# Linear attention beside a top-8 MLP on one core: q computed token-major and transposed by DMA, M built mostly in one pass, first outputs copied out by ScalarE

## The chip, the cores and the metric

The kernel runs on one core of one Trainium2 chip. The metric is the device time of one execution, in microseconds (us); lower is better. Inside the core, TensorE (PE in the profile, its weight loads PEld) multiplies, VectorE (DVE), ScalarE (ACT) and GpSimd (POOL) do elementwise work, and SyncE (SP) issues most of the DMAs. Matmul results land in PSUM, in eight banks of 128 x 512 float32.

## The reference, cut to what matters

The input x has 2048 tokens of 640 columns. The output is `x + A(layernorm(x)) + B(layernorm(x))`.

```
# A: linear attention, 32 heads of 20 columns
q, k, v = split(xn @ wqkv)                 # [32 heads, 2048, 20] each
phi(t) = where(t > 0, t + 1, exp(t)) + 1e-6
kv  = sum_s phi(k)[s]^T v[s]               # one 20 x 20 block per head
z   = sum_s phi(k)[s]
num = phi(q) @ kv ;  den = phi(q) . z + 1e-6
A   = concat_heads(num / den) @ wo
# B: eight tokens, chosen by r, go through an MLP
r = xn @ w_r ;  idx = the 8 largest of r
y = (silu(xn[idx] @ w_gate) * (xn[idx] @ w_up)) @ w_down * sigmoid(r[idx])
B = xn, with y added to the rows idx
```

## The kernel before, in words

Tokens are worked in 16 tiles of 128 (`T = 16`); the 640 columns are five groups of 128 (`KC = 5`). There is no scheduler: the order on each engine is the order in which the code is written, and each engine works through its own list in order. SP's list is the DMA queue of nearly all transfers. Buffers are tiles of pools; an instruction that writes a PSUM tile waits for the instructions that read that tile before, and the waits are made per tile, not per column.

**Start.** Ten wide matmuls on zeros (`warm_mm`, L271) run while the first tokens arrive. Tiles 0 to 2 of the normalised input are transposed by PE, tiles 3 to 15 by DMA (`ln_norm`, L196: `xnT<-xn`).

**Loop over tiles.** For tile t PE does `k_mm` (token-major, matmuls of 512 and 129 columns, L236), `ga_mm(t - 1)` (three matmuls into the running sum G = xn^T phi(k), L259) and `q_mm` (L248: 25 matmuls of 128 columns, weights as the stationary operand with a column step of 5, so that q comes out already transposed, [column, token]). ScalarE takes exp and relu of k and q from PSUM, VectorE joins them to phi: `pk` for k (token-major) and `pqT` for q (transposed, written straight by VectorE, L225). `late_loads(t)` puts one weight load per tile on SP; `keep` writes finished rows of `x + xn` to a DRAM buffer `xcp` (L363).

**After the loop.** PE transposes r for the top-8 search (`pr`, L428), sums phi(k) over the tokens (`z_mm`, L460), continues G in `gb1` (L489), merges the top-8 candidates (`pc`, L499), and when `gb1` is through it forms the denominators (`pden`, L571) from `pqT` and `zm`. `zm` holds z spread over heads; z gets from rows to partitions by four small DMAs (`zrel`, L477). ScalarE turns den into 1/den (`rden`, L580, L581); it goes to DRAM in four copies and back as `rb`, and VectorE multiplies `pqT` by it in four blocks of 512 tokens (`norm(j)`, L632). Between these stand the MLP's first half (`gu`, L606), the last part of G (`gb2`, L590), the head blocks of kv (`pkv`, L659, evicted under a mask by VectorE, L670) and the MLP's second half (`py`, L688). `py` is scattered into `xcp` by an indirect DMA (L697), and `x_sb` is read back from there in six pieces (L702).

**M.** M = kv @ wo is built in five row groups m (L728). Each needs two passes over wo, of even and odd blocks of 80 rows, in four 32-column strips of PE; each M group is copied to SBUF by ScalarE or VectorE (L737).

**Outputs.** For each tile, ten matmuls (five groups m, columns 0 to 511 and 512 to 639, L743), an add of `x_sb` by VectorE straight from PSUM (L751), and a DMA to the output. Four PSUM accumulators take turns: three pairs of banks and the two single banks D0 and D1.

Of the kernel before, what the change touches and what calls it, by code (L numbers as in the profile page):

```python
# [25 lines left out]
PAD = 16  # L26
# [3 lines left out]
WARM = 10  # L30
LAST = (0, 320, 512, 640)
# [13 lines left out]
def kernel(  # L45
# [47 lines left out]
    kvT = sb([EB, PAD + NEB * KC * 2 * PAD], BF16, "kvT")  # L93
# [4 lines left out]
    rscr = dram.tile([NTB * P, TBLK], BF16, name="rscr")  # L98
# [32 lines left out]
    headg = sb([P, NTB, H], BF16, "headg")  # L131
    nc.vector.memset(headg[:], 1.0)
    mask80 = sb([EB, KC, 4, 4], BF16, "mask80")
# [20 lines left out]

    head_select(headg[:], [(0, NTB), (-4, H)], 1, 4)
# [87 lines left out]

    def q_mm(t, tag="B"):
        ps = pair(tag, f"q{t}")
        for m in range(KC):
            for kc in range(KC):
                nc.tensor.matmul(  # L248
                    ps[:, m * P : (m + 1) * P],
                    lhsT=wq[:, kc, m::KC],  # L250
                    rhs=xnT[:, kc, t * P : (t + 1) * P],
                    start=(kc == 0 and m in (0, 4)), stop=(kc == KC - 1),
                    skip_group_check=True,
                )
        return ps
# [47 lines left out]
    def small_consts(t):  # L303
        if t == 3:
            for j in range(4):
                nc.gpsimd.affine_select(
                    out=cmask[:], in_=cmask[:], compare_op=ALU.not_equal, fill=1.0,
                    base=-32 * j, pattern=[[-1, C]], channel_multiplier=1,
                )
        elif t == 4:  # L310
            nc.gpsimd.affine_select(
                out=selm[:], in_=selm[:], compare_op=ALU.not_equal, fill=1.0,
                base=0, pattern=[[-1, NTB]], channel_multiplier=1,
            )
            nc.gpsimd.iota(iota_i[:], pattern=[[1, 32]], base=0, channel_multiplier=0)
            nc.gpsimd.tensor_copy(iof[:], iota_i[:])
        elif t == 5:
            nc.gpsimd.iota(prt_i[:, 0:1], pattern=[[0, 1]], base=4 * S, channel_multiplier=1)
            nc.gpsimd.iota(prt_i[:, 1:2], pattern=[[0, 1]], base=0, channel_multiplier=TBLK)
            nc.gpsimd.tensor_copy(prt[:], prt_i[:])  # L320
            nc.gpsimd.tensor_copy(boff[:], prt[0:NTB, 1:2])
        elif t == 6:
            head_select(mask80[:], [(0, KC), (-DH, 4), (0, 4)], 1, DH)
# [17 lines left out]
    def late_loads(t):  # L341
        def part(dst, src, a, b):
            nc.sync.dma_start(dst[:, a:b, :], src[:, a:b, :])

        wv_v = wqkv_v[:, :, 2 * D : 3 * D]
        plan = {
            2: (x_sb, x_v, 8, 12), 5: (x_sb, x_v, 12, 16),
            6: (wg, kcF, 0, 2), 7: (wg, kcF, 2, 4), 8: (wg, kcF, 4, 5),
            9: (wu, kcU, 0, 2), 10: (wu, kcU, 2, 4), 11: (wu, kcU, 4, 5),
            12: (wv, wv_v, 0, 2), 13: (wv, wv_v, 2, KC), 14: (wo, wo_v, 0, 4), 15: (wo, wo_v, 4, 8),  # L350
            16: (wd, kcD, 0, 6), 17: (wd, kcD, 6, 12),
        }
        if t in plan:
            part(*plan[t])

# [12 lines left out]
    def q_phi(t, er):  # L368
        phi_vec(pqT[:, :, t * P : (t + 1) * P], er, True)
# [72 lines left out]
    nc.vector.max(cand[:, 0, :], rT[:])  # L442
    nc.vector.max_index(idxu[:], cand[:, 0, :], rT[:])
# [13 lines left out]
    def z_mm(t):  # L457
        i = t % 4
        for a, b in ((0, TBLK), (TBLK, D)):
            nc.tensor.matmul(  # L460
                zp[32 * i : 32 * i + 32, a:b],
                lhsT=ones_bf[:],
                rhs=pk[:, t, a:b],
                start=(t < 4), stop=(t >= T - 4),
                tile_position=(0, 32 * i),
            )
# [5 lines left out]
    zpart = sb([P, D], F32, "zpart", tag="rb")  # L472
    nc.scalar.copy(zpart[:], zp[:, 0:D])
# [6 lines left out]
    late_loads(T)  # L480
    late_loads(T + 1)
# [25 lines left out]
    for t in range(4, T):  # L507
        gb1(t)
# [22 lines left out]
    q_phi(T - 1, qer)  # L531
# [4 lines left out]
    for c in range(C):  # L536
# [7 lines left out]
        out=zm[:], in0=headg[:, 0, :].unsqueeze(1).to_broadcast([P, KC, H]),  # L544
# [19 lines left out]
    keep(T - 4, T)  # L564
    nc.scalar.copy(GT[:, 3:5, 0:TBLK], two(gbA[:]))
# [15 lines left out]
    nc.scalar.activation(rden[:], lden[:], AF.Exp, scale=-1.0)  # L581

# [14 lines left out]

    for t in range(2):
        gb2(t)
# [3 lines left out]
    for a, w in enumerate((wg, wu)):  # L603
# [15 lines left out]
    rb = sb([P, S], BF16, "rb")  # L619

    nc.sync.dma_start(
        rscr[:].rearrange("(p r) n -> p r n", r=4), rden[:].unsqueeze(1).to_broadcast([P, 4, TBLK])
    )
    for j in (0, 2):
        nc.sync.dma_start(
            rb[:, j * TBLK : (j + 2) * TBLK].rearrange("p (j n) -> p j n", j=2),
            rscr[j * P : (j + 2) * P, :].rearrange("(j p) n -> p j n", j=2),
        )

    def norm(j):  # L630
        sl = pqT[:, :, j * TBLK : (j + 1) * TBLK]
        nc.vector.tensor_tensor(  # L632
            out=sl, in0=sl,
            in1=rb[:, j * TBLK : (j + 1) * TBLK].unsqueeze(1).to_broadcast([P, KC, TBLK]),
            op=ALU.mult,
        )

    for t in range(2, 12):
# [9 lines left out]
    for t in range(12, T):  # L648
        gb2(t)
    nc.scalar.copy(GT[:, :, TBLK:D], gbC[:, 0:D].rearrange("p (c f) -> p c f", c=KC))  # L650


    pkv = (bank("D0", "pkv0"), bank("D1", "pkv1"), pair("B", "pkv2"))
    groups = ((0, 2, 4), (1, 3, 5), (6, 7))

    def kv_mm(i):
        for n, b in enumerate(groups[i]):
# [9 lines left out]
    def kv_evict(i):  # L667
        n, w = len(groups[i]), KC * 2 * PAD
        lo, step = groups[i][0], groups[i][1] - groups[i][0]
        nc.vector.tensor_tensor(  # L670
            out=kvT[:, PAD : PAD + NEB * w].rearrange("e (b m c) -> e b m c", b=NEB, m=KC)[
                :, lo : groups[i][-1] + 1 : step, :, 0:PAD
            ],
            in0=pkv[i][0:EB, 0 : n * EB].rearrange("e (b c m) -> e b m c", b=n, m=KC),
            in1=mask80[:].rearrange("e m h j -> e m (h j)").unsqueeze(1).to_broadcast([EB, n, KC, PAD]),
            op=ALU.mult,
        )

    for i in range(3):
        kv_mm(i)  # L680
        kv_evict(i)
# [21 lines left out]

    M = sb([P, KC, D], BF16, "M", tag="wq")
    halves = ((0, TBLK), (TBLK, D))

    class Acc:
        def __init__(self, tag, name):
            if tag == "D":
                self.banks = bank("D0", name + "a"), bank("D1", name + "b")  # L710
                self.spans = halves
            else:
                self.banks = (pair(tag, name),)
                self.spans = ((0, D),)
# [7 lines left out]
    for m in range(KC):  # L722
        pm = Acc("CBADC"[m], f"M{m}")
        for a, b in halves:
            for i in range(2):
                for g in range(4):
                    o = PAD + ((2 * g + i) * KC + m) * 2 * PAD - i * PAD
                    nc.tensor.matmul(  # L728
                        pm.at(a, b)[32 * g : 32 * g + 32, :],
                        lhsT=kvT[:, o : o + 2 * PAD],  # L730
                        rhs=wo[:, 2 * g + i, a:b],
                        start=(i == 0), stop=(i == 1),
                        tile_position=(0, 32 * g),
                    )
        copy = nc.vector.tensor_copy if m in (2, 4) else nc.scalar.copy
        for a, b in pm.spans:
            copy(M[:, m, a:b], pm.at(a, b))  # L737
    norm(1)
    norm(2)


    def out_mm(t, ps, m, a, b):
# [4 lines left out]
            start=(m == 0), stop=(m == KC - 1),  # L747
# [5 lines left out]
    for t in range(T):  # L753
        o_t = work.tile([P, D], BF16, tag=("ek", "rk", "eq", "rq")[t % 4], name=f"o_t{t}")
        if t < T - 1:
            po = Acc("BADC"[t % 4], f"o{t}")
            for m in range(KC):
# [5 lines left out]
            if t == 4:  # L763
                norm(3)
        else:
            for i in range(3):
                a, b = LAST[i : i + 2]
                ps = pair("CBA"[i], f"o_last{i}")[:, 0 : b - a]
                for m in range(KC):
# [37 lines left out]
```

## Time and profile before

| | |
|---|---|
| median of 3 runs | 111.77 us (111.38 to 111.93) |
| the profiled execution: time | 111.62 us |
| its span, first to last instruction | 109.9 us |
| PE busy share of the span | 96% |
| DVE, ACT, POOL busy share | 78%, 50%, 34% |
| DMA: bytes moved, mean rate | 23.09 MB, 210 GB/s |
| granted PE clock | 1.00 |

The profile comes from one execution; the 1.7 us between its span and its time are start and end of the program. Times in the views are counted from the span's first instruction. Matmuls overlap in their pipeline, so the mean duration of one (381 ns for 512 columns) is longer than the distance between two; that distance is read from the chain of waits.

### The profile page before, as it was taken

The numbers are of one execution on the slowest core, as the hardware profiler recorded it, in microseconds if no ns is written. First come the engines' busy times: TensorE is split into PE (matmuls) and PEld (weight loads), VectorE is DVE, ScalarE is ACT, GpSimd is POOL, SyncE is SP. The second block draws the span as 40 slices with busy tenths as digits, with TensorE's granted clock in tenths as the row PEclk, the third lists the DMA queues.
The fourth block names the chain that finished last, engine by engine and source line by source line (L and its number), as shares of the span: only waits on it lengthen the run. The fifth ranks groups of instructions, "written<-read, shape, count | busy, mean of one in ns | idle before, by whom it ended". The sixth has DMA issues, their size and how long they took to land.

```text
span 109.9 us, 2999 instructions
## 1 busy us (share of the span) xinstructions
PE 105.5 (96%) x1183; PEld 69.3 (63%) x1183; DVE 86.1 (78%) x205; ACT 55.1 (50%) x102; POOL 37.9 (34%) x83
## 2 busy tenths in 40 slices
PE   6998999999999999999999999999999999999990
PEld 2456866777577766777667744447995555555560
DVE  6889999887999889875999896951348967698680
ACT  4037987778867797777977745068028000000000
POOL 5414195989889955770000000240008100000000
DMA  2998164930569999998859970899541289997333
GB/s 72 335 375 292 33 36 75 283 66 3 118 177 321 220 267 280 316 305 224 290 187 285 292 257 5 232 378 372 175 145 51 15 228 323 340 387 277 128 119 119
DMA packets 25358, 23.09 MB, mean 210 GB/s; under 512 B 10624, under 2 KB 24064, under 8 KB 25344
## 3 DMA queue, kind: packets, MB, share of 16 engines
q1 hardware_dynamic: 22784, 20.43, 66.5%
q10 hardware_dynamic: 2384, 2.43, 6.4%
q8 instruction: 9, 0.15, 0.6%
q0 software_dynamic: 176, 0.04, 0.6%
q14 instruction: 5, 0.04, 0.1%
HBM read 14.94 MB, written 5.81 MB: 189 GB/s over the span
## 4 chain that ended last, share of the span: by engine, by line
PE 76%; DVE 10%; POOL 8%; issue 3%; DVEq 0%; POOLq 0%
PE o L743 14%; PE k L236 13%; PE q L248 13%; PE gbA L489 6%; PE gaC L259 5%; PE warm L271 4%; PE gbC L590 4%; POOL sq L176 3%; DVE st L163 2%; PE gaD L259 2%; DVE pk L225 2%; PE M L728 2%; POOL sc L178 2%; DVE xn L191 2%; PE gu L606 2%
## 5 line engine op out<-in xcount | busy, mean ns | idle before, releaser
L248 PEld LDWEIGHTS <-wq 128*128 128x128 bf16 x400 | 24.2, 117 | 3.4
L236 PE MATMUL k<-wk,xnT 128*128 128x512 bf16 (+1 forms) x160 | 24.8, 301 | 0.3 <-ACT xnT L206 0.3
L248 PE MATMUL q<-xnT,wq 128*128 128x128 bf16 x400 | 24.9, 220 | 0.0
L743 PEld LDWEIGHTS <-pqT 128*128 128x128 bf16 x165 | 12.8, 98 | 9.3
L236 PEld LDWEIGHTS <-xnT 128*128 128x128 bf16 x160 | 12.3, 98 | 8.5 <-ACT xnT L206 0.9
L213 ACT ACTIVATE eq<-q 128x640 bf16<-128x640 f32 x16 | 11.2, 703 | 10.5 <-PE q L248 10.5
L225 DVE SCALAR_TENSOR_TENSOR pk<-ek,rk 128x640 bf16<-128x640 bf16 x16 | 13.2, 824 | 3.6 <-ACT rk L216 3.4
L743 PE MATMUL o<-M,pqT 128*128 128x512 bf16 x110 | 15.8, 300 | 0.0
L176 POOL TENSOR_TENSOR sq<-sq,half 128x1 bf16<-128x1 bf16 x16 | 12.5, 778 | 6.2 <-DVE sc L175 4.0
L163 DVE BATCH_NORM_STATS2 st<-x_sb 128x6 f32<-128x320 bf16 x32 | 14.1, 480 | 0.4 <-DMA x_sb<-in_A_x_dram 0.4
L225 DVE SCALAR_TENSOR_TENSOR pqT<-eq,rq 128x640 bf16<-128x640 bf16 x16 | 13.2, 823 | 0.7 <-ACT rq L216 0.7
L213 ACT ACTIVATE ek<-k 128x640 bf16<-128x640 f32 x16 | 11.3, 705 | 1.6 <-PE k L236 0.4
L751 DVE TENSOR_TENSOR o_t<-o,x_sb 128x640 bf16<-128x640 f32 x11 | 8.8, 820 | 3.3 <-DMA x_sb<-xcp 1.7
L216 ACT ACTIVATE rq<-q 128x640 bf16<-128x640 f32 x16 | 11.2, 700 | 0.0
L216 ACT ACTIVATE rk<-k 128x640 bf16<-128x640 f32 x16 | 11.2, 699 | 0.0
L259 PE MATMUL gaC<-pk,xn 128*128 128x512 bf16 x32 | 9.5, 378 | 0.2 <-DVE pk L225 0.2
L537 POOL COPY xsT<-xnT 128x5 bf16 x8 | 1.9, 312 | 21.7 <-DVE icol L551 21.7
L178 POOL TENSOR_TENSOR sc<-sq,neg 128x1 f32<-128x1 bf16 x12 | 8.6, 716 | 0.9
L191 DVE TENSOR_SCALAR xn<-x_sb,sc 128x640 bf16<-128x640 bf16 (+2 forms) x17 | 6.9, 412 | 1.2 <-POOL sc L179 1.0
L489 PE MATMUL gbA<-pk,xn 128*128 128x512 bf16 x32 | 7.3, 380 | 0.0
L360 DVE TENSOR_TENSOR x_sb<-x_sb,xn 128x640 bf16<-128x640 bf16 x16 | 7.0, 482 | 0.0
L259 PEld LDWEIGHTS <-xn 128*128 128x128 bf16 x48 | 4.0, 97 | 4.1 <-issue 0.4
(152 smaller groups left out, 120.4 us busy)
## 6 DMA issues: line engine op xcount, KB each, us to landing
xcp<-x_sb SPq DMA_DIRECT2D x4, 640.0 KB, 5.2
x_sb<-in_A_x_dram SPq DMA_DIRECT2D x3, 640.0 KB, 4.7
wd<-in_B_w_down_dram SPq DMA_DIRECT2D x2, 960.0 KB, 6.6
x_sb<-xcp SPq DMA_DIRECT2D x3, 640.0 KB, 6.8
wg<-in_B_w_gate_dram SPq DMA_DIRECT2D x2, 768.0 KB, 6.6
wu<-in_B_w_up_dram SPq DMA_DIRECT2D x2, 768.0 KB, 5.3
out_dram<-o_t ACTq DMA_DIRECT2D x8, 160.0 KB, 2.7
out_dram<-o_t SPq DMA_DIRECT2D x7, 160.0 KB, 3.4
```

Source lines behind the costliest of these rows:

```text
L163: nc.vector.bn_stats(out=stat[t][:, h, :], in_=x_sb[:, t, h * HW : (h + 1) * HW])
L176: nc.gpsimd.tensor_tensor(out=sq[:, 1:2], in0=sq[:, 0:1], in1=half[:], op=ALU.pow)
L178: nc.gpsimd.tensor_tensor(out=sc[:, 1:2], in0=sq[:, 1:2], in1=neg1[:], op=ALU.pow)
L191: nc.vector.tensor_scalar(out=xn[:, t, a:b], in0=x_sb[:, t, a:b], scalar1=sc[:, 0:1], scalar2=sc[:, 1:2], op0=ALU.subtract, op1=ALU.mult,)
L213: nc.scalar.activation(e[:], ps[:, 0:D], AF.Exp)
L216: nc.scalar.activation(r[:], ps[:, 0:D], AF.Relu)
L225: nc.vector.scalar_tensor_tensor(out=dst, in0=ea, scalar=1.0, in1=ra, op0=ALU.min, op1=ALU.add)
L236: nc.tensor.matmul(ps[:, a:b], lhsT=xnT[:, kc, t * P : (t + 1) * P], rhs=wk[:, kc, a:b], start=(kc == 0), stop=(kc == KC - 1),)
L248: nc.tensor.matmul(ps[:, m * P : (m + 1) * P], lhsT=wq[:, kc, m::KC], rhs=xnT[:, kc, t * P : (t + 1) * P], start=(kc == 0 and m in (0, 4)) ...
L259: nc.tensor.matmul(gaC[:, c * TBLK : (c + 1) * TBLK] if c < 2 else gaD[:], lhsT=xn[:, t, c * P : (c + 1) * P], rhs=pk[:, t, 0:TBLK], start ...
L489: nc.tensor.matmul(gbA[:, (c - 3) * TBLK : (c - 2) * TBLK], lhsT=xn[:, t, c * P : (c + 1) * P], rhs=pk[:, t, 0:TBLK], start=(t == 0), stop ...
L743: nc.tensor.matmul(ps, lhsT=pqT[:, m, t * P : (t + 1) * P], rhs=M[:, m, a:b], start=(m == 0), stop=(m == KC - 1),)
```

## The change

- **q.** `q_mm` makes q token-major, like k: for each of the five groups the normalised tile is the stationary operand, and `wq` is streamed in 512 and 128 columns. `regroup` orders the columns: of each head of 20 the first 8, the next 8 and the last 4, so that column groups 0 to 3 hold eights of 16 heads each and group 4 the fours of all heads. The streamed operand is therefore read in runs of 8 (or 4) elements at a step of 20. phi(q) goes to a buffer `pq` (three of them), and SP transposes it by DMA into `pqT`: 16 more DMA transposes. `z_mm` streams `pk` in the same order.
- **Order.** phi of q's last tile moves ahead in VectorE's list, into the search for candidates. `pden` stands after `gb1` of tile 12 (`DEN_AT = 13`), and `gb1` of tiles 13 to 15 follows it. The loads of `wv` move to tiles 8 and 11, those of `wd` from behind the loop to tiles 12 and 13. Two of the four `zrel` DMAs stay on SP, two go on ScalarE's queue.
- **Reciprocals.** `rden` goes to DRAM once, and `rb` is read back in three partition orders, 12 DMAs of 128 x 512; `rb` shares the buffer of `xnT`. `norm(j)` takes two multiplications.
- **kv and M.** kv comes in two groups of four blocks, each evicted in three VectorE instructions. M's groups 0 to 3 take one pass, group 4 two, in the order 0, 2, 1, 3, 4. Groups 0 and 2 share the pair of banks C; the last 128 columns of groups 0 to 3 lie in the second bank of pair A beside group 1's 512 columns; group 4 has pair B.
- **Outputs.** The accumulator of tiles t with t mod 4 = 0 is bank D1 and columns 640 to 767 of pair B; with t mod 4 = 3 it is bank D0 and columns 0 to 127 of the same pair B; the others are the pairs C and A. The first five tiles (`NPRE = 5`) are copied out by ScalarE, and VectorE adds `x_sb` in SBUF.

```diff
     def q_mm(t, tag="B"):
         ps = pair(tag, f"q{t}")
-        for m in range(KC):
-            for kc in range(KC):
+        for kc in range(KC):
+            for rhs, a, b in regroup(wq[:, kc, :]):
                 nc.tensor.matmul(
-                    ps[:, m * P : (m + 1) * P],
-                    lhsT=wq[:, kc, m::KC],
-                    rhs=xnT[:, kc, t * P : (t + 1) * P],
+                    ps[:, a:b],
+                    lhsT=xnT[:, kc, t * P : (t + 1) * P],
+                    rhs=rhs,
...
+    def regroup(ap):
+        v = ap.rearrange("p (h e) -> p h e", e=DH)
+        main = v[:, :, 0 : 2 * E8].rearrange("p h (c d) -> p c h d", c=2)
+        return (main, 0, TBLK), (v[:, :, 2 * E8 : DH], TBLK, D)
...
     def q_phi(t, er):
-        phi_vec(pqT[:, :, t * P : (t + 1) * P], er, True)
+        pq = work.tile([P, D], BF16, tag="pq", name=f"pq{t}", bufs=3)
+        phi_vec(pq[:], er, False)
+        nc.sync.dma_start_transpose(pqT[:, :, t * P : (t + 1) * P], pq[:])
...
-            12: (wv, wv_v, 0, 2), 13: (wv, wv_v, 2, KC), 14: (wo, wo_v, 0, 4), 15: (wo, wo_v, 4, 8),
-            16: (wd, kcD, 0, 6), 17: (wd, kcD, 6, 12),
+            12: (wd, kcD, 0, 6), 13: (wd, kcD, 6, 12), 14: (wo, wo_v, 0, 4), 15: (wo, wo_v, 4, 8),
...
+        if t == 8:
+            part(wv, wv_v, 0, 2)
+        elif t == 11:
+            part(wv, wv_v, 2, KC)
...
     nc.vector.max(cand[:, 0, :], rT[:])
+    q_phi(T - 1, qer)
     nc.vector.max_index(idxu[:], cand[:, 0, :], rT[:])
...
-            (nc.sync if i < 3 else nc.scalar).dma_start(
+            (nc.sync if i < 2 else nc.scalar).dma_start(
...
-    for t in range(4, T):
+    for t in range(4, DEN_AT):
         gb1(t)
...
+    for t in range(DEN_AT, T):
+        gb1(t)
+    nc.scalar.copy(GT[:, 3:5, 0:TBLK], two(gbA[:]))
...
+    mC, mA, mB = pair("C", "M02"), pair("A", "M1r"), pair("B", "M4")
+    mD, mE = bank("D0", "M3"), bank("D1", "oX")
+    m_at = (mC, 0), (mA, 0), (mC, TBLK), (mD, 0), (mB, 0)
+    m_rest = tuple((mA, TBLK + m * P) for m in range(4)) + ((mB, TBLK),)
...
+    m_pass(0)
+    m_copy(nc.scalar.copy, 0)
+    m_pass(2)
+    m_copy(nc.scalar.copy, 2)
+    m_pass(1)
+    m_copy(nc.vector.tensor_copy, 1)
+    m_pass(3)
+    m_copy(nc.scalar.copy, 3)
+    m_pass(4, 0)
+    m_pass(4, 1)
...
     class Acc:
-        def __init__(self, tag, name):
-            if tag == "D":
-                self.banks = bank("D0", name + "a"), bank("D1", name + "b")
+        def __init__(self, t):
+            k = t % 4
+            if k in (1, 2):
+                self.banks = (pair("?CA"[k], f"o{t}"),)
+                self.spans = ((0, D),)
+            else:
+                lo = TBLK + P if k == 0 else 0
+                self.banks = (mE if k == 0 else mD)[:], mB[:, lo : lo + P]
                 self.spans = halves
...
+    for t in range(NPRE):
...
+        o_pre[t] = o_tile(t)
+        for a, b in acc[t].spans:
+            nc.scalar.copy(o_pre[t][:, a:b], acc[t].at(a, b))
+    for t in range(NPRE):
+        nc.vector.tensor_tensor(out=o_pre[t][:], in0=o_pre[t][:], in1=x_sb[:, t, :], op=ALU.add)
+        (nc.scalar, nc.sync)[t % 2].dma_start(out_v[:, t, :], o_pre[t][:])
+    norm(3)
```

More of the change, by code (lines that the diff above doesn't have):

```diff
@@ L130 @@
     nc.vector.memset(kvT[:], 0.0)
[L131 to L133 removed]
+    headm = sb([P, KC, NV, HV], BF16, "headm")
+    nc.vector.memset(headm[:], 0.0)
+    for m in range(4):
+        nc.vector.memset(headm[:, m, m % 2, :], 1.0)
+    nc.vector.memset(headm[:, 4], 1.0)
+    mask80 = sb([EB, 4, E8], BF16, "mask80")
     nc.vector.memset(mask80[:], 1.0)
@@ L617, with rb_load, norm @@
     nc.vector.tensor_tensor(out=hm[:], in0=gu[:, TBLK : TBLK + FJ], in1=hm[:], op=ALU.mult)
[L619 to L627, printed above, removed]
-        )
[L630 to L638, printed above, removed]
+    rb = sb([P, NV + 1, S], BF16, "rb", tag="xnT")
+    def rb_load(j):
+        lo = j * TBLK
+        for v in range(NV + 1):
+            h0, n, r = (v * HV, HV, E8) if v < NV else (0, H, E4)
+            nc.sync.dma_start(
+                rb[:, v, lo : lo + TBLK],
+                rscr[32 * j + h0 : 32 * j + h0 + n, :].unsqueeze(1).to_broadcast([n, r, TBLK]),
+            )
+    nc.sync.dma_start(rscr[:], rden[:])
+    keep(T - 4, T)
+    for j in range(NTB):
+        rb_load(j)
+    def norm(j):
+        js = slice(j * TBLK, (j + 1) * TBLK)
+        sl = pqT[:, 0:4, js].rearrange("p (c v) n -> p c v n", v=NV)
+        nc.vector.tensor_tensor(
+            out=sl, in0=sl, in1=rb[:, 0:NV, js].unsqueeze(1).to_broadcast([P, 2, NV, TBLK]), op=ALU.mult
+        )
+        nc.vector.tensor_tensor(out=pqT[:, 4, js], in0=pqT[:, 4, js], in1=rb[:, NV, js], op=ALU.mult)
+    for t in range(12):
         gb2(t)
@@ L647 @@
     )
[L648 to L654, printed above, removed]
+    pkv = bank("D0", "pkv0"), bank("D1", "pkv1")
     def kv_mm(i):
-        for n, b in enumerate(groups[i]):
+        for n in range(4):
+            b = 4 * i + n
             for kc in range(KC):
@@ L667, in kv_evict @@
     def kv_evict(i):
[L668 to L681, printed above, removed]
+        src = pkv[i][0:EB, 0 : 4 * EB].rearrange("e (b h c) -> e b h c", b=4, h=4)
+        main = kvT[:, 256 * i : 256 * (i + 1)].rearrange("e (b c h d) -> e c b h d", b=4, c=2, h=4)
+        rest = kvT[:, 512 + 128 * i : 512 + 128 * (i + 1)].rearrange("e (b x) -> e b x", b=4)
+        for c in range(3):
+            w = E8 if c < 2 else E4
+            dst = main[:, c] if c < 2 else rest[:, :, 0:16].rearrange("e b (h d) -> e b h d", h=4)
+            nc.vector.tensor_tensor(
+                out=dst, in0=src[:, :, :, c * E8 : c * E8 + w],
+                in1=mask80[:, :, 0:w].unsqueeze(1).to_broadcast([EB, 4, 4, w]), op=ALU.mult,
+            )
+    for t in range(12, 14):
+        gb2(t)
+    kv_mm(0)
+    kv_evict(0)
+    for t in range(14, T):
+        gb2(t)
+    nc.scalar.copy(GT[:, :, TBLK:D], gbC[:, 0:D].rearrange("p (c f) -> p c f", c=KC))
     norm(0)
@@ L767 @@
                 a, b = LAST[i : i + 2]
-                ps = pair("CBA"[i], f"o_last{i}")[:, 0 : b - a]
-                for m in range(KC):
+                ps = (mD, mB, mE)[i][:, 0 : b - a]
+                for m in M_ORDER:
                     out_mm(t, ps, m, a, b)
```

129 lines of the change are left out of this document (79 added, 50 removed).

## The prediction

> **What bounds the kernel now.** I read the page's first and fourth parts, then the chain in order of time, then a table by stretches of time and the groups by shape. First the page: busy shares by engine, and the shares of the chain that ended last.
>
> ```profile
> PE 105.5 (96%) x1183; PEld 69.3 (63%) x1183; DVE 86.1 (78%) x205; ACT 55.1 (50%) x102; POOL 37.9 (34%) x83
> ...
> PE 76%; DVE 10%; POOL 8%; issue 3%; DVEq 0%; POOLq 0%
> ```
>
> PE is busy nearly throughout. The chain (start, duration, what) shows the distance between matmuls, which their own durations hide:
>
> ```profile
> 1.05 4.77 PE warm L271 x13
> ...
> 57.66 1.40 PE q L248 x25
> 59.05 1.38 PE k L236 x10
> ...
> 61.09 1.40 PE q L248 x25
> ...
> 66.60 0.13 PE pc L499
> 66.73 0.02 PE pc L503
> 66.74 5.29 PE gbA L489 x24
> 72.03 1.19 PE pden L571 x20
> ...
> 79.81 1.53 PE pkv L659 x40
> 81.34 0.94 PE py L688 x48
> 82.28 1.63 PE M L728 x48
> ...
> 85.00 2.82 PE o L743 x20
> ```
>
> From tile 6 to the end PE follows PE. So the time falls only where PE gets less work, and rises by every new wait of PE in its own order. PE is not the only full resource. Columns here: stretch, busy time by engine, clock, DMA share, GB/s.
>
> ```profile
> 28.00:30.00 2.00, 1.77 (x13) 0.91 (x11) 2.00 (x4) 1.91 (x4) 1.79 (x7) 1.00 0.71 142
> 31.00:55.20 24.20, 24.20 (x274) 17.63 (x272) 20.70 (x44) 18.57 (x35) 14.28 (x25) 1.00 1.08 272
> 55.20:56.20 1.00, 1.00 (x13) 0.68 (x11) 1.00 (x3) 0.54 (x1) 0.00 (x0) 1.00 0.03 12
> 56.20:65.20 9.00, 9.00 (x114) 5.91 (x113) 8.44 (x17) 6.44 (x13) 0.00 (x0) 1.00 1.02 306
> 69.00:75.50 6.50, 6.50 (x85) 3.16 (x82) 3.76 (x14) 3.19 (x4) 1.94 (x8) 1.00 1.00 332
> 36.30:38.00 1.70, 1.70 (x25) 1.36 (x24) 1.36 (x3) 1.46 (x4) 1.54 (x5) 1.00 1.39 152
> 43.00:46.00 3.00, 3.00 (x37) 2.22 (x35) 2.51 (x6) 2.23 (x6) 2.61 (x4) 1.00 1.11 359
> ```
>
> From 31 to 65 us the DMA engines are full but for one microsecond. Nobody on PE waits for them today, because what they carry is needed late. The change puts 16 transposes and two weight loads into this stretch, and makes PE need the last of them.
>
> **The change part by part.** The sum is made against the profiled execution's 111.62 us, 0.15 below the median of the runs.
>
> *q, gain 0.34.* 25 matmuls at 1.40 become ten like k's, which take 1.38 with one column more; 0.021 by 16 tiles. The streamed operand is now strided. The only strided read in the trace is q's old weight load:
>
> ```profile
> L248 PEld LDWEIGHTS <-wq 128*128 128x128 bf16 x400 | 24.2, 117 | 3.4
> L743 PEld LDWEIGHTS <-pqT 128*128 128x128 bf16 x165 | 12.8, 98 | 9.3
> ```
>
> A step of five elements made it 117 against 98 ns. Were the stream slowed by the same 19%, q would cost 16 x 0.26 = 4.2 us more; below zero it can't cost. Runs of eight are nearer to the contiguous row, so I take nothing. [...]
>
> *M, gain 1.09, then loss of 1.45.* The old M takes 85.00 - 82.28 = 2.72, ten passes of 0.272. The new one has six: 1.63. But the accumulators are shared, and waits are per tile. Pass 2 writes the pair that ScalarE is copying group 0 from; the last 128 columns of pass 3 go to the pair that VectorE copies group 1 from.
>
> ```profile
> L737 ACT CAST M<-M3a 128x512 bf16<-128x512 f32 x1 | 0.6, 585 | 0.2 <-PE M3a L728 0.2
> L737 ACT CAST M<-M3b 128x128 bf16<-128x128 f32 x1 | 0.3, 272 | 0.0
> L751 DVE TENSOR_TENSOR o_t<-o10a,x_sb 128x512 bf16<-128x512 f32 x1 | 0.7, 692 | 0.0
> L751 DVE TENSOR_TENSOR o_t<-o10b,x_sb 128x128 bf16<-128x128 f32 x1 | 0.3, 280 | 0.0
> ```
>
> A copy begins 0.2 after PE's last matmul. First wait: 0.2 + 0.585 + 0.05 for the signal, less 0.06 for the 128 columns that PE still has: 0.78. Second: 0.2 + 0.692 + 0.05 less 0.27: 0.67. M becomes 3.08, a net loss of 0.36.
>
> *Outputs, loss 2.4.* Tiles with t mod 4 of 3 and 0 follow each other and now share pair B. So the second matmul of tiles 4, 8 and 12 waits until the tile before is read out, with ten matmuls queued behind it. At tile 4 ScalarE reads: 0.14 + 0.585 + 0.272 - 0.1 (they overlap) + 0.05, less the 0.22 of the one matmul ahead: 0.73. At 8 and 12 VectorE reads: 0.14 + 0.692 + 0.28 - 0.08 + 0.05 - 0.22, about 0.85 each. Sum 2.43. The old rotation had D0 and D1 as a tile's own banks, and the chain has no such wait. ScalarE's five copies cost nothing: it is idle after M. VectorE must be level again by tile 7 for the 0.85 to hold, and x_sb comes late:
>
> ```profile
> 94.34 0.82 DVE L751 TENSOR_TENSOR o_t<-o,x_sb 128x640 bf16<-128x640 f32 x1 [0.86 <-DMA x_sb<-xcp]
> 95.08 1.48 DVE L632 TENSOR_TENSOR pqT<-pqT,rb 128x2560 bf16<-128x2560 bf16 x1
> ```
>
> Tile 4's rows came 9.3 after the outputs' start at 85.00. Half of kv (0.77) and the longer M (0.36) now stand between py and the outputs, so 8.2. One add (under 0.82), norm(3) at 1.48 and two adds of 0.82 end at about 12.1 or sooner; PE ends tile 7 at 8 x 1.36 + 0.73 = 11.6 and its readout starts 0.2 later. So it holds, barely: each microsecond that x comes later is one more at tile 8.
>
> *The candidates, loss 0.3.* phi of the last q goes before the search ends:
>
> ```profile
> L225 DVE SCALAR_TENSOR_TENSOR pqT<-eq,rq 128x640 bf16<-128x640 bf16 x16 | 13.2, 823 | 0.7 <-ACT rq L216 0.7
> 65.75 0.21 DVE L437 TENSOR_TENSOR candm<-split,selm 4x64 bf16<-4x64 bf16 x1
> 70.18 0.33 DVE L543 TENSOR_TENSOR zm<-headg,zc 128x160 bf16<-128x160 bf16 x1
> 67.69 1.18 SPq L343 DMA_DIRECT2D wd<-in_B_w_down_dram  x2
> 49.51 1.21 SPq L196 DMA_TRANSPOSE xnT<-xn  x1
> ```
>
> The candidates were ready at 65.96, PE took them at 66.60 (pc): 0.64 of cover for 0.82 of new work, and 0.1 for the signal. Queued behind pc stand gb1 and all that follows.
>
> *The denominators, loss 4.0.* They are moved ahead by three tiles of gb1 (5.29/12 = 0.44 each): PE would be there at 72.03 - 1.32 - 0.34 + 0.3 = 70.7. They need the last transposed q and zm, hence zrel, two of whose DMAs stand on SP behind that transpose. Ahead of these in SP's queue: transposes of tiles 4 to 14 and the last one, and both wd. The wd pair is 1.97 MB, at 375 GB/s (between 359 and a full queue) 5.2 us. A transpose moves 0.164 MB. At 359 GB/s that is 0.46; in 28:30 two of them held the engines for 0.71 x 2.0 = 1.42, 0.71 each; in 36.3:38.0 one took the whole 1.7 at 152 GB/s. I take 0.6, between the first two, since most should be queued with others: 12 x 0.6 = 7.2. Against it stand the idle microsecond at 55 and three stretches like 36.3:38.0, which a deeper queue can fill, about 1.1 each: 4.3 in all. The queue then runs dry at 65.2 - 0.3 + 12.4 - 4.3 = 73.0 instead of 65.2; landing and sum over rows 1.1, zm 0.6: 74.7. PE waits 4.0, with gb1, the MLP and all the rest queued behind. Ends: with 0.46 a transpose 2.3; with 1.1 a transpose 10.
>
> [...]
>
> *Answered with one line each.* On SP a transpose takes 1.21 to issue and a load 0.59 (half of the wd row), so a tile's issues are 3.0 us within its 3.43 (61.09 - 57.66); xnT is still made three tiles ahead. GpSimd's extra masks fit, it is idle two thirds of the time. The reciprocals come back in 12 DMAs; norm(0) needs the first three, some 2 us of issues at a load's 0.59, and PE has 9 us of other work between pden's end and M to cover that; without the cover norm(0) would hold the outputs. kv's six evictions instead of three lie under py and the second half of kv.
>
> Sum: 111.62 - 0.34 + 0.36 + 2.43 + 0.3 + 4.0 = 118.4.
>
> **The rivals.**
> - *The queue keeps up*: the transposes slip between the weight loads, as the xnT ones do in 43:46 at 359 GB/s, and nothing is late for the denominators. Then only the PSUM waits are left: 114.4. Against it: share 1.08 over 24 us.
> - *The queue starves the loop*: every pair of transposes behaves like 36.3:38.0. Then even xnT comes late, k waits, and the end slips by 6 more: 124. For it: three such stretches among seven transposes; against it: what is queued behind them could fill the gaps.
> - *The clock falls*: the warm-up's ten matmuls of 512 and three of 128 columns take 4.77 in the chain's first row, 0.44 for 512 columns, where k's ten later take 1.38, 0.22 for 512; so PE runs at half pace when it comes from idling. [...]
> - *Faster*: the waits for shared PSUM are not taken, because the readers are done before PE comes back. It decides at a lag of readout below 0.2 us behind PE; then M and q give 1.43 and the queue keeps up: 110.2. Against it: the copies' own durations above.
> - A change without effect would need losses of 1.4 exactly; I see no mechanism.
>
> **How the numbers follow.** Forecast (denominators late by 2 to 6) 0.50, queue keeps up 0.18, clock falls 0.14, loop starves 0.11, faster 0.04, near no change 0.03. About 0.5%, 0.56 us, is what a measurement can tell from no change. So faster 0.04, same 0.03, slower 0.93. The time is the forecast's, 118.4 on the profiled execution, 118.5 on the median's footing. The range runs from the queue keeping up, 114.4, to just short of the starved loop, 123.
>
> **What would show it.** Right: a wait on PE before pden with a DMA of zrel or pqT as its end; waits of 0.7 to 0.9 at the second matmul of tiles 4, 8, 12; two in M; q at 1.38 a tile. Wrong: pden starting right behind gb1 of tile 12, or q's matmuls further apart than k's, or no gap at tile 8.

## The result, and the profile after

The changed kernel takes 127.65 us (median of 4 runs, 127.47 to 129.24) against 111.69 for the kernel before (111.38 to 111.93): a ratio of 1.146, 95% interval 1.137 to 1.156. The prediction was 118.5, with a range from 114.4 to 123. The profiled execution took 127.47 us with a span of 125.7; that of before, 111.62 with 109.9. The 15.8 us between the spans are what has to be found.

First the page of the changed kernel: busy shares, then the granted clock in 40 slices, then the shares of the chain that ended last, by engine and by line.

```profile
PE 107.4 (85%) x899; PEld 58.9 (47%) x911; DVE 84.7 (67%) x217; ACT 59.9 (48%) x111; POOL 36.8 (29%) x91
...
PEclk9999999999999999999999999559999999999999
...
PE 65%; DMA 13%; DVE 10%; issue 4%; ACT 3%; SPq 2%; ACTq 0%; DVEq 0%
PE k L242 15%; PE q L259 12%; DMA xnT<-xn 9%; PE o L800 7%; PE warm L281 4%; PE gbC L611 4%; DMA zrel<-zpart 3%; PE gaC L269 3%; PE M L800 3%; PE gbA L510 3%; PE oX L800 3%; DVE o_t L809 3%; PE gaD L269 2%; PE pden L589 2%; SPq L389 2%
```

PE was busy for 96% of the span and is now busy for 85%: it waits. DMAs, which had no share of the chain, hold 13% of it, and two slices in the middle show a clock of half speed. Next the chain in order of time (start, duration, what), to be laid beside the rows of before in the prediction.

```profile
55.55 7.10 DMA xnT<-xn
62.66 0.05 issue
62.70 1.56 PE k L242 x10
...
64.91 1.41 PE q L259 x10
66.33 0.32 PE pr L448 x4
...
70.50 0.17 PE pc L520
...
75.42 0.60 SPq L500
76.02 0.05 issue
76.08 4.31 DMA zrel<-zpart
...
81.14 2.52 PE pden L589 x15
83.66 1.37 PE gbA L510 x3
...
94.75 0.36 PE M L747 x4
...
98.07 0.32 PE oX L800
```

And what PE waited for (who waited for whom: us in total, times, longest):

```profile
PE pden L589 <- DVE zm L563: 6.5, 1, 6.5
PE k L242 <- DMA xnT<-xn: 3.3, 4, 1.5
PE M L800 <- DVE o_t L809: 1.5, 2, 0.8
...
PE M L747 <- ACT M L758: 0.6, 1, 0.6
PE M1r L747 <- DVE M L758: 0.6, 1, 0.6
PE M L800 <- ACT o_t L834: 0.6, 1, 0.6
```

One row of before was not shown yet, the start of the transposes of r, which ends the loop:

```profile
62.48 0.32 PE pr L428 x4
```

From these starts the whole difference can be set out by stretches. Three tiles of `gb1` moved from ahead of `pden` to behind it; 1.32 us are moved back for them.

| stretch | before | after | difference | predicted |
|---|---|---|---|---|
| start to `pr` (the loop) | 62.48 | 66.33 | +3.85 | -0.34 |
| `pr` to `pc` | 4.12 | 4.17 | +0.05 | +0.3 |
| `pc` to `pden`, without the three tiles | 4.11 | 10.64 | +6.53 | +4.0 |
| `pden` to M, with the three tiles | 11.57 | 13.61 | +2.04 | 0 |
| M | 2.72 | 3.32 | +0.60 | +0.36 |
| outputs to the end of the span | 24.9 | 27.63 | +2.73 | +2.43 |

The rows add up to 15.80. M and the outputs came nearly as forecast. The loop, the wait for `pden` and the stretch behind it came 8.8 us worse (4.19 + 2.53 + 2.04), and the experiments ask for the cause of these first.

### The profile page after: what moved, and what is told of

Read it like the earlier page. It is cut to its first block, busy times and chain, and to the rows that moved or that the text cites. A ratio compares the mean times of both kernels' runs of the same rounds, so it can differ in the third digit from the quotient of the medians.

```text
span 125.7 us, 2535 instructions
## 1 busy us (share of the span) xinstructions
PE 107.4 (85%) x899; PEld 58.9 (47%) x911; DVE 84.7 (67%) x217; ACT 59.9 (48%) x111; POOL 36.8 (29%) x91
## 3 DMA queue, kind: packets, MB, share of 16 engines
q10 hardware_dynamic: 2528, 2.43, 5.8%
## 4 chain that ended last, share of the span: by engine, by line
PE 65%; DMA 13%; DVE 10%; issue 4%; ACT 3%; SPq 2%; ACTq 0%; DVEq 0%
PE k L242 15%; PE q L259 12%; DMA xnT<-xn 9%; PE o L800 7%; PE warm L281 4%; PE gbC L611 4%; DMA zrel<-zpart 3%; PE gaC L269 3%; PE M L800 3%; PE gbA L510 3%; PE oX L800 3%; DVE o_t L809 3%; PE gaD L269 2%; PE pden L589 2%; SPq L389 2%
## 5 line engine op out<-in xcount | busy, mean ns | idle before, releaser
L259 PE MATMUL q<-wq,xnT 128*128 128x512 bf16 (+1 forms) x160 | 25.2, 303 | 0.0
L242 PEld LDWEIGHTS <-xnT 128*128 128x128 bf16 x160 | 12.2, 98 | 14.5 <-DMA xnT<-xn 4.8
L259 PEld LDWEIGHTS <-xnT 128*128 128x128 bf16 x160 | 12.9, 96 | 11.9
L231 DVE SCALAR_TENSOR_TENSOR pq<-eq,rq 128x640 bf16<-128x640 bf16 x16 | 13.1, 818 | 2.2 <-DMA pqT<-pq 1.5
L800 PE MATMUL o<-M,pqT 128*128 128x512 bf16 (+1 forms) x78 | 12.2, 297 | 0.2
L800 PE MATMUL M<-M,pqT 128*128 128x128 bf16 (+3 forms) x60 | 9.5, 268 | 2.0 <-DVE o_t L809 1.5
L269 PE MATMUL gaC<-pk,xn 128*128 128x512 bf16 x29 | 8.8, 378 | 0.0
L557 POOL COPY xsT<-xnT 128x5 bf16 x8 | 1.1, 210 | 24.6 <-DMA wo<-in_A_wo_dram 24.6
L589 PE MATMUL pden<-pqT,zm 128*32 128x512 bf16 x20 | 2.5, 626 | 6.5 <-DVE zm L563 6.5
L510 PE MATMUL gbA<-pk,xn 128*128 128x512 bf16 x30 | 7.9, 403 | 0.1
L721 POOL DMA_INDIRECT xcp<-y_sb,rowu x1 | 1.8, 1752 | 18.9 <-DVE pqT L659 18.9
```

What stands on the lines that cost most here:

```text
L231: nc.vector.scalar_tensor_tensor(out=dst, in0=ea, scalar=1.0, in1=ra, op0=ALU.min, op1=ALU.add)
L242: nc.tensor.matmul(ps[:, a:b], lhsT=xnT[:, kc, t * P : (t + 1) * P], rhs=wk[:, kc, a:b], start=(kc == 0), stop=(kc == KC - 1),)
L259: nc.tensor.matmul(ps[:, a:b], lhsT=xnT[:, kc, t * P : (t + 1) * P], rhs=rhs, start=(kc == 0), stop=(kc == KC - 1),)
L269: nc.tensor.matmul(gaC[:, c * TBLK : (c + 1) * TBLK] if c < 2 else gaD[:], lhsT=xn[:, t, c * P : (c + 1) * P], rhs=pk[:, t, 0:TBLK], start ...
L510: nc.tensor.matmul(gbA[:, (c - 3) * TBLK : (c - 2) * TBLK], lhsT=xn[:, t, c * P : (c + 1) * P], rhs=pk[:, t, 0:TBLK], start=(t == 0), stop ...
L800: nc.tensor.matmul(ps, lhsT=pqT[:, m, t * P : (t + 1) * P], rhs=M[:, m, a:b], start=(m == M_ORDER[0]), stop=(m == M_ORDER[-1]), skip_group ...
```

## The experiments

Queue landings given below without a row are the landing times of single DMAs in the trace; "the last keep" is the third write of finished rows to `xcp`, the last large transfer ahead of `zrel`.

**1. No added transposes** (`e1_q_from_pe`): q by stationary weights, as before.

```
-        for kc in range(KC):
-            for rhs, a, b in regroup(wq[:, kc, :]):
+        for m in range(KC):
+            for kc in range(KC):
...
+                    lhsT=wq[:, kc, m::KC],
...
-        phi_vec(pq[:], er, False)
-        nc.sync.dma_start_transpose(pqT[:, :, t * P : (t + 1) * P], pq[:])
+        phi_vec(pqT[:, :, t * P : (t + 1) * P], er, True)
```

> The changed kernel with q made as before: weights stationary, q lands transposed, VectorE writes phi(q) straight to its place, and the 16 added transposes are gone. The columns come in the old order (step of five), so the grouping by heads is left out; every other edit of the change stays. Theory (the 16 transposes fill the DMA queue; late xnT, late zrel and the fallen clock all follow from that): the loop's 4.15 us, the wait of 6.5 before pden and the 2.0 of half clock all go, 127.65 - 12.65 = 115.0 us, between 114.3 and 115.7. Rival (the early wd and wv loads and the order of the queue do it, the transposes only add to it): half of it stays, 119 to 123.

Measured: 115.54 us (115.04 to 117.84), ratio to before 1.033, interval 1.029 to 1.037. In its chain the loop ends at the time of before and `pden` follows `gb1` without a gap, at full clock (1.00):

```profile
62.30 0.32 PE pr L447 x4
...
66.66 3.99 PE gbA L509 x18
70.65 1.19 PE pden L588 x20
71.84 1.40 PE gbA L509 x6
```

The early `wd` and `wv` loads are still in this kernel, and nothing waits for them. So without the 16 transposes nothing of the losses ahead of M is left, and the rival, by which half would stay, falls. That does not make `wd` free: beside the transposes it has a price of its own (experiment 4). This edit also changes how q is multiplied and stored; experiment 2 adds transposes and nothing else.

**2. The transposes alone** (`e5_transposes_alone`): put into the kernel before, for nobody.

```
         phi_vec(pqT[:, :, t * P : (t + 1) * P], er, True)
+        if t < T - 1:
+            nc.sync.dma_start_transpose(spare[t % 4][:], pk[:, t, :])
```

> The kernel before with one edit: behind phi(q) of tiles 0 to 14 SP issues a DMA transpose of the same tile of phi(k) into a spare buffer that nobody reads. Eleven of the 15 fall behind 31 us. Theory (a transpose costs the full queue 0.7 to 0.85 us, and nothing of it is hidden): the queue runs dry at 65.2 + 8 to 9, zrel comes at 74 to 75, pden at about 75.5 instead of 72.0, and wd and the reciprocals behind it come late too: 116 to 119, taken 117.5. Rival of the prediction (gaps take 4.3 of it): 113. Rival (transposes cost only because their reader waits, pqT before pden): 112.

Measured: 117.15 us (116.78 to 118.36), ratio 1.051, interval 1.045 to 1.058. The last keep landed at 75.55 instead of 66.54, so the eleven transposes that land behind 31 us cost the queue 9.0 us, 0.82 each (the next expectation has 75.3 and 0.80). PE waits for xnT in the loop (1.5 us in two waits) and 3.1 before `pden`. Transposes that nobody reads do the same kind of harm as those of the change.

**3. The same bytes without transposing** (`e11_copies_alone`): plain copies in the same places.

```
-            nc.sync.dma_start_transpose(spare[t % 4][:], pk[:, t, :])
+            nc.sync.dma_start(spare[t % 4][:], pk[:, t, :].rearrange("p (k f) -> p k f", k=KC))
```

> The kernel before with 15 plain DMA copies of phi(k) into the spare buffers, 0.164 MB each, in the places where the run with transposes alone had its 15 transposes (there the last keep landed at 75.3 instead of 66.5: 8.75 us for the 11 behind 31 us, 0.80 each, and the time was 117.15). Theory (it is the transposing that is dear, not the bytes or the place in the queue): a copy costs 0.164 MB at 359 GB/s, 0.46 us, the last keep lands near 71.5, pden waits 1 us or less, 113 to 114.5. Rival (any transfer put into a full queue costs 0.8, by being small or by holding up what is behind it): last keep near 75, time 116.5 to 117.5.

Measured: 111.99 us (111.29 to 112.73), ratio 1.003, interval 1.001 to 1.006. The last keep landed at 68.44: 1.9 us for eleven copies, 0.17 each, where their bytes alone are 0.46 each at 359 GB/s. That is less than the theory had (71.5). Two stretches of each kernel side by side, first with transposes, then with copies (stretch, busy time by engine, clock, DMA share, GB/s):

```profile
31.00:55.00 24.00, 22.48 (x246) 16.01 (x244) 19.58 (x42) 17.21 (x32) 13.62 (x25) 1.00 1.09 238
55.00:66.00 11.00, 11.00 (x138) 7.69 (x139) 9.46 (x18) 7.96 (x15) 0.00 (x0) 1.00 1.11 276
```

```profile
31.00:55.00 24.00, 24.00 (x271) 17.43 (x268) 20.50 (x43) 18.44 (x35) 14.38 (x25) 1.00 1.11 292
55.00:66.00 11.00, 11.00 (x135) 7.22 (x134) 10.36 (x23) 7.42 (x15) 0.00 (x0) 1.00 1.08 345
```

The share of busy time is the same, 1.08 to 1.11; the rate is not. Before the change it was 272 GB/s in the first stretch: copies raise it to 292, transposes lower it to 238. A full queue had room for more bytes, but not for more transposes.

**4. The loads of wd behind `zrel`** (`e2_wd_behind`):

```
-            12: (wd, kcD, 0, 6), 13: (wd, kcD, 6, 12), 14: (wo, ...
+            16: (wd, kcD, 0, 6), 17: (wd, kcD, 6, 12), 14: (wo, ...
...
+    late_loads(T)
+    late_loads(T + 1)
```

> The changed kernel with the two loads of wd put back behind the loop, behind zrel in the queue. Theory (bytes and engine time of the queue): wd's 5.2 us leave the queue ahead of zrel, the wait before pden goes from 6.5 to about 1.3 us and the clock doesn't fall: 127.65 - 5.2 - 2.0 = 120.4, between 119.5 and 122. The loop stays late, since wd comes behind the last xnT. Rival (SP's own time for issuing is the limit, not the engines): only the two issues of 0.58 are saved, 126.5.

Measured: 121.57 us (119.89 to 123.53), ratio 1.080, interval 1.071 to 1.089. `pden` begins at 74.91 after a wait of 2.3 and the clock stays at 1.00. A part is given back in a place that the expectation left out: `rden` now stands behind `wd` in the queue.

```profile
74.91 1.48 PE pden L591 x20
...
77.79 4.55 DMA rscr<-rden
...
83.13 3.34 DMA rb<-rscr
...
86.57 1.29 DVE pqT L658
```

The write of the reciprocals takes 4.55 us to land (in the changed kernel 1.8), and norm(0) at 86.57 waits for what is read back. The saving ahead of `pden` is that of the engines' time: the last of `zrel` lands at 74.2, and at 78.3 in the unchanged kernel with the same loop (experiment 7). That is 4.1 for `wd`; two issues of 0.58 would have been 1.2. Another pair of rows speaks against the rival too. Two of the four `zrel` DMAs of the changed kernel don't pass through SP, and before the change one did not (last number: median us from issue to landing; first before, then after the change):

```profile
zrel<-zpart ACTq DMA_DIRECT2D x1, 2.5 KB, 2.1
zrel<-zpart ACTq DMA_DIRECT2D x2, 2.5 KB, 5.7
```

Issued from ScalarE's queue, 2.5 KB still take 5.7 us: the backlog is not SP's alone. SP is slow as well. From 57 us on it takes 1.8 to 3.0 us to issue a transpose of q, where the prediction reckoned with 1.21, and until 76.7 it never rests for more than 0.6 us. Those five transposes land 6.0 to 8.7 us after their issue. Whether the full queue is what slows the issues, no run separates.

**5. PE kept busy during the wait** (`e3_keep_warm`): 28 matmuls on zeros ahead of `pden`.

```
+    warm2 = bank("D0", "warm2")
+    for _ in range(28):
+        nc.tensor.matmul(
+            warm2[:], lhsT=zero[:], rhs=zero[:, 0:1].to_broadcast([P, TBLK]), start=True, stop=True
+        )
     pden = bank("D0", "pden")
```

> The changed kernel with 28 matmuls on zeros (512 columns, 0.22 us each, 6.1 us in all) put on PE just ahead of pden, where it idles for 6.5 us. Theory (idling lowers the granted clock): pden takes 1.2 instead of 2.5 us and gb1 behind it 1.3 instead of 2.0, 127.65 - 2.0 = 125.6. Rival (pden is slow by itself in its new place, by reading fresh transposes or sharing banks): nothing changes, 127.6, pden still 2.5.

```profile
80.40 1.47 PE pden L594 x20
81.87 1.40 PE gbA L510 x6
83.27 1.74 PE gu L629 x40
```

`pden` and the three tiles take 2.87 instead of 4.53 us: 1.66 of the expected 2.0. The granted clock is 1.00 over both rows, where the changed kernel has 0.50 during `pden` and 0.70 during the three tiles. The time is 126.74 us (125.11 to 126.93), ratio 1.131, interval 1.124 to 1.139; that the saving shows in it can't be said, since the changed kernel itself came out at 127.65 and at 125.89 (experiment 7). The trace is the evidence here.

**6. A shorter idle stretch** (`e9_short_idle`): the same with 9 matmuls.

> The changed kernel with 9 matmuls on zeros ahead of pden instead of 28: PE works 2.0 us more and idles some 4.4 of the 6.4 us. Known so far: after 1.8, 2.3 and 3.1 us of idling pden took 1.3 to 1.5, after 6.4 to 6.7 it took 2.5. Theory (the clock falls after a fixed idle window between 3.1 and 4.4): pden 2.5 again. Rival (the window is longer, or what counts is the share of a longer stretch): pden 1.2 to 1.5.

Measured once: 125.31 us. PE idled for 4.5 us; `pden` took 2.09 and the three tiles 2.42, 4.51 together, as much as after 6.5 us of idling. The clock in steps of half a microsecond (the clock is the third column from the end), first of this kernel, then of the changed one:

```profile
79.00:79.50 0.50, 0.50 (x10) 0.44 (x14) 0.43 (x4) 0.00 (x0) 0.00 (x0) 1.00 0.00 0
79.50:80.00 0.50, 0.50 (x12) 0.40 (x8) 0.47 (x3) 0.00 (x0) 0.00 (x0) 0.69 0.05 16
...
83.00:83.50 0.50, 0.50 (x6) 0.07 (x8) 0.00 (x0) 0.00 (x0) 0.00 (x0) 0.90 0.27 94
```

```profile
77.50:78.00 0.50, 0.00 (x0) 0.00 (x0) 0.00 (x0) 0.00 (x0) 0.00 (x0) 1.00 1.04 387
78.00:78.50 0.50, 0.00 (x0) 0.00 (x0) 0.00 (x0) 0.00 (x0) 0.00 (x0) 0.54 1.07 399
84.50:85.00 0.50, 0.50 (x2) 0.19 (x2) 0.00 (x0) 0.50 (x1) 0.00 (x0) 0.63 0.00 0
```

A slice with 0.69 is at half speed for 62% of its length, so here the clock falls at 79.69 and is back at 83.10: 3.41 us. In the changed kernel it falls at 78.04 and is back at 84.87: 6.83, twice as long. With 9 matmuls it falls 0.7 us after PE has taken up work again, 5.2 us after the gap began; in the changed kernel it falls 3.4 us after the gap began. Three more profiles, with gaps of 6.4 to 6.7 us (experiments 7, 8 and 9), have the fall 3.2 to 4.4 us into the gap and 6.82 or 6.83 us long. So the fall keeps no fixed distance from the start of the gap, which the theory's window would have needed, and it lasts 3.41 us or twice that. What sets its start and its length these runs do not show: 3.1 us of idling (experiment 2) brought no fall, 4.5 and more did, and the 0.7 us of matmuls just ahead of the fall did not keep it off here. `pden` and the three tiles took 4.3 to 5.1 us in the three other profiles, so the price of a fall varies too.

**7. The changed kernel again** (`c1_after_again`), unchanged:

> The changed kernel unchanged, as a second look beside the others. In two kernels with the same loop, PE reached the transposes of r at 64.2 and 64.7 us instead of 66.3, and pden still began near 80. Theory (the DMA queue sets pden's start, so the loop's lateness and the wait before pden are one loss and not two): pr between 64 and 66.5, pden between 79.5 and 81.2, time 127 to 128. Rival (two separate losses): where pr comes two earlier, pden comes two earlier as well.

Measured: 125.89 us (125.33 to 128.18), ratio 1.123, interval 1.117 to 1.130. `pr` at 64.26, the wait before `pden` 6.4, `pden` at 79.04. The loop came 2.1 earlier than in the first profile and `pden` came 2.1 earlier with it, as the rival has it. But the queue as a whole ran earlier:

```profile
54.37 6.23 DMA xnT<-xn
...
74.00 4.29 DMA zrel<-zpart
```

The last xnT lands at 60.60 instead of 62.66 and the last `zrel` at 78.29 instead of 80.39, 2.1 earlier at both places. So the theory's fixed start of `pden` is refuted, but the run does not tell whether a later loop would lengthen the sum or only move a loss from one wait to the other. What it shows is that both places follow the queue. How much of the loss falls into the loop varies: 1.3 us of waits for xnT here, 3.3 there.

**8. q's stream without strides** (`e6_q_contiguous`):

```
-            for rhs, a, b in regroup(wq[:, kc, :]):
+            for rhs, a, b in ((wq[:, kc, 0:TBLK], 0, TBLK), (wq[:, kc, TBLK:D], TBLK, D)):
```

> The changed kernel with q's streamed operand read in the plain order of columns, 512 and 128 in a row; the grouping by heads is left out. Theory (the strided stream costs a little): the chain's distance of q goes from 1.42 to 1.38, 0.6 us over 16 tiles, nothing of it seen in the time since the queue sets it. Rival (the 1.42 is something else, such as sharing PE with the strided store of ScalarE): it stays 1.42.

Measured once: 125.5 us. In the chain q's ten matmuls take 1.36, on every tile, where the changed kernel has 1.42:

```profile
30.46 1.36 PE q L259 x10
```

Runs of eight (and four) at a step of 20 cost 0.06 per tile, 0.9 over 16. Token-major q read in a row would have gained 0.04 a tile on the old 1.40; as it is read it loses 0.02.

**9. Accumulators of their own** (`e4_own_banks`): M's groups in C, B, A, D0 with D1, and C again; outputs in turn as before.

```
-    mC, mA, mB = pair("C", "M02"), pair("A", "M1r"), pair("B", "M4")
-    mD, mE = bank("D0", "M3"), bank("D1", "oX")
+    mC, mA, mB = pair("C", "M0"), pair("A", "M1"), pair("B", "M2")
+    mD, mE = bank("D0", "M3a"), bank("D1", "M3b")
...
+            if k == 2:
+                self.banks = bank("D0", f"o{t}a"), bank("D1", f"o{t}b")
+            else:
+                self.banks = (pair("BA?C"[k], f"o{t}"),)
```

> The changed kernel with an accumulator of its own for each M group and each output tile in turn: groups 0, 2, 1, 3, 4 in pairs C, B, A, banks D0 and D1, pair C, outputs rotating B, A, D0 and D1, C as before. Theory (PSUM shared, waits made per tile): M's two waits of 0.75 and the outputs' 0.57, 0.75 and 0.71 go, 3.5 in all, 124.1. Rival (VectorE is behind anyway because x_sb and norm(3) come late, so PE only waits elsewhere): M's 1.5 go and the outputs keep theirs, 126.1.

Measured: 122.47 us (121.96 to 123.37), ratio 1.097, interval 1.092 to 1.103. The loop again ended earlier (64.66), so the share of the edit is read from M's start: to the end of the span it is 27.7 us (120.8 - 93.08) instead of 30.95, so 3.2 of the expected 3.5 are back, and the rival falls. From the outputs on PE follows PE:

```profile
93.08 1.05 PE M L747 x24
94.16 0.70 ACT M L761
94.90 0.73 PE M L747 x16
95.63 2.82 PE o L801 x20
99.81 4.08 PE o L801 x30
```

One wait of 0.6 stays in M, for the fifth group, which takes the first one's pair. Why ScalarE's copy of the first group began only at 94.16, 0.8 after its last matmul, is open.

**10. Both repairs, and versions meant to win.** `e10_pe_q_own` has q by stationary weights in all tiles and accumulators with no reuse inside M: groups in C, B, A, D0 and D1, the last 128 columns of groups 3 and 4 beside group 1.

```
+    m_at = (mC, 0), (mA, 0), (mB, 0), (mD, 0), (mE, 0)
+    m_rest = (mC, TBLK), (mA, TBLK), (mB, TBLK), (mA, TBLK + P), (mA, TBLK + 2 * P)
```

> The changed kernel with q of all tiles by stationary weights (old order of columns, the grouping by heads left out), no added transposes, and the same accumulators as in the kernel beside it. Theory (the kernel without transposes took 115.5; M's two waits of 0.75 and the outputs' 0.57, 0.75, 0.71 are all that separates it from the kernel before, plus the gain of 1.09 in M): 115.5 - 3.5 = 112.0, and M's distance is 1.65. Rival (the single-pass M only moves its cost to the copies, which the outputs then wait for): 113 to 114.

Measured: 111.82 us (111.11 to 112.79), ratio 0.9995, interval 0.997 to 1.002: all that the change lost is back, and it is level with the kernel before.

```profile
83.17 0.66 PE M L746 x16
...
84.91 4.30 PE o L797 x30
```

M takes 1.74 (84.91 - 83.17) instead of 2.72: the single pass does earn 0.98 of its 1.09. In this profile M begins 0.9 later than before, 0.4 of it by a wait for zm, and from the outputs to the end of the span it takes 25.5 us instead of 24.9; so it ends level. PE's part of these 0.6 is 0.2; the rest lies behind its last matmul, and its cause is open.

`e7_mix_own` keeps the order by heads: q of tiles 0 to 3 by transposes, of the others from a copy of `wq` that GpSimd groups.

```
+        if t >= Q_TR:
...
+                        lhsT=wqg[:, kc, m * P : (m + 1) * P],
...
+                    nc.gpsimd.tensor_copy(
+                        dst[:, c * 256 : (c + 1) * 256].rearrange("p (h d) -> p h d", d=E8), src[:, c]
+                    )
```

> A version meant to beat both: the changed kernel with q of tiles 0 to 3 as in the change (token-major, DMA transposes, early, when the queue has room) and q of tiles 4 to 15 with weights stationary as before, from a copy of wq whose columns GpSimd has grouped by heads; and with the accumulators not shared (C, B, A, D0 and D1). Theory: no queue loss, M 2.55 instead of 2.72, outputs without waits: 111.0 to 112.0, taken 111.4. Rival (the copies on GpSimd hold up the normalisation of tiles 5 to 7, whose powers GpSimd takes): the loop slips, 112.5 to 114.

Measured: 117.33 us (116.23 to 118.22), ratio 1.040, interval 1.035 to 1.046; a miss. The copies stand on GpSimd ahead of the powers of the normalisation, and PE pays:

```profile
PE gaC L294 <- DVE pk L232: 2.6, 2, 2.2
PE q L274 <- POOL wqg L263: 1.8, 1, 1.8
```

`e8_no_waits` spreads the copies over ScalarE, VectorE and GpSimd in tiles 2 to 4 and takes M's banks of `e10_pe_q_own`.

```
+        if t == 2:
+            wq_group(nc.scalar.copy, 0, 2, 0)
+        elif t == 3:
+            wq_group(nc.scalar.copy, 2, 4, 0)
+            wq_group(nc.vector.tensor_copy, 0, 2, 1)
+            wq_group(nc.gpsimd.tensor_copy, 0, KC, 2)
...
```

> Second try at a version that beats both: q of tiles 0 to 4 token-major with early DMA transposes, q of tiles 5 to 15 with weights stationary from a copy of wq grouped by heads, made in seven small copies spread over ScalarE's and VectorE's gaps of tiles 2 to 4 and one on GpSimd; M's groups in C, B, A, D0, D1, the last 128 columns of groups 3 and 4 beside group 1 in A and copied at the end; outputs rotating C, B, A, D0 with D1. Theory: no queue loss, no wait in M (1.63 instead of 2.72), none in the outputs, a few tenths for the early transposes: 110.5 to 111.5, taken 111.0. Rival (the early copies and transposes hold up the first tiles, as GpSimd's did): 112 to 114.

Measured: 111.60 us (110.97 to 112.77; the kernel before, measured beside it, 111.6), ratio 0.9997, interval 0.997 to 1.003. It keeps the order by heads and the single-pass M without the cost of the change, and is no faster than before by anything that these runs can tell. No version beat the kernel before.

## Why the prediction was wrong

**The denominators: the step that failed.** The prediction put a transpose at 0.6 us, twelve of them in the way of the denominators, and took off 4.3 us because an idle microsecond and three thin stretches would be filled. The 4.3 taken off is what failed. For a transpose by itself 0.6 was about right: of the ten that experiment 2 issues behind 31 us, eight land 0.53 to 0.81 us behind the transfer ahead of them. But on balance nothing was filled: eleven held up the queue by 9.0 us, 0.82 each, where the step as it was worked gives 11 x 0.6 - 4.3 = 2.3. Experiment 3 shows that there were gaps, since plain copies cost 0.17 of their 0.46. The thin stretches were no room for another transpose, because a transpose was in them. The row 36.30:38.00 in the prediction said so, full share at 152 GB/s, and was read as room.

The packets of the kernel before agree with that: between 31 and 55 us, 72 of the 4480 packets of transposes (256 bytes each) stand for over 0.2 us, where the median is 18 ns, and these 72 make up 4.8 of the 9.9 us for which transposes keep an engine busy on average. What they stand waiting for is not shown. Against this `wd` was dearer in the prediction (5.2) than on the chip (4.1). With the measured prices the prediction's own sum has 12 x 0.82 + 4.1 in place of 7.2 - 4.3 + 5.2 and puts `pden` 5.8 us later, at 80.5 instead of 74.7; that is an estimate after the fact, and the two profiles of the changed kernel have 81.14 and 79.04.

The low end of the prediction, 0.46 us a transpose at 359 GB/s, does not hold beside loads: 0.164 MB in 0.82 us is 200 GB/s.

**The loop: a rival that came as well.** "xnT is still made three tiles ahead" counted SP's issues, at 1.21 each, and not the landings. The transposes of xn stand behind those of q and the loads, and PE waits for them: 3.3 us in the first profile, 1.3 in the second. The rest of the 3.85 is q's 1.42 instead of 1.40 (0.3) and slow first matmuls after each wait (k at 1.56 instead of 1.38, four times), less some 0.4 that the kernel before loses early in the loop to a wait for pk.

**The clock: another.** The stretch behind the wait is 2.0 longer, and experiment 5 takes back 1.66 of it; the prediction had a falling clock among its rivals, with a chance of 0.14.

**So the three were not rivals.** The prediction gave the starved loop 0.11 and the clock 0.14 as alternatives to the late denominators. All three follow from one cause, a queue that is slower than thought (experiment 1 removes them together), and came together: 3.85 + 6.53 + 2.04, where 4.0 less 0.34 was forecast. That is why the time lies beyond the range.

**What held.** The outputs: waits of 0.57, 0.75 and 0.71 at tiles 4, 8 and 12 against 0.73, 0.85 and 0.85. M's two waits came, at 0.6 each against 0.78 and 0.67, and it lost 0.60 against 0.36. The waits were put too long by the lag of the reader: the 0.2 in the prediction's rows is how long ScalarE had been idle, not how long after PE's last matmul the copy began (in the kernel before that is 0.06, 84.40 behind 84.34); without the lag of 0.14 the sums for the outputs give 0.59 and 0.72. M lost more all the same, because its passes are longer than 1.63 (1.74 without waits, experiment 10, and slow first matmuls after a wait: 0.40 for the four at 95.77, where experiment 10 has 0.22). VectorE was level by tile 7, just: it began to read tile 7 0.04 us after PE's last matmul. phi of the last q inside the search cost 0.05 and not 0.3. The reciprocals in 12 DMAs were covered, as forecast. q's gain of 0.34 was a loss of 0.3, and its matmuls further apart than k's are a sign that the prediction itself had named as wrong: the strided stream, bounded at 0 to 4.2, cost 0.9, and the prediction took 0.

## What to carry to other kernels

Before adding transfers to a queue that shows a full share, look at the bytes per second in the same rows: a full share at half the rate (here 1.39 at 152 GB/s, beside 1.11 at 359) is not room. Price each kind of transfer by its own thin rows, and add nothing back for gaps that the same kind made. And when several rivals have one cause, give them one chance and add up their prices.

## What was not expected of the hardware

- A DMA transpose of 128 x 640 bf16 among weight loads costs the queue 0.82 us net; a plain copy of the same bytes costs it 0.17 net (experiments 2 and 3).
- In the five profiles that show one, the clock's fall lasts 3.41 or 6.82 to 6.83 us, and begins 3.2 to 5.2 us after PE has fallen idle; a wait of 4.5 us cost as much as one of 6.5 (4.51 and 4.53 us for the same work).
- A matmul stream in runs of 8 (or 4) elements at a step of 20 is 4% slower than one in a row (1.42 against 1.36 for ten matmuls).
- GpSimd's copies of 128 x 256 and 128 x 128 bf16 into grouped order, between the powers of the normalisation, held PE up for over 4 us (waits of 2.6 and 1.8 in `e7_mix_own`).
